# A gated recurrence followed by a long FFT convolution: weight scaling and sine arguments on GpSimd, spectral products on VectorE, a new instruction order

## Chip, core and metric

The kernel runs on one core of a Trainium2 chip, as one program. The core has five engines with a queue each: TensorE (PE in the profile, with its weight loads as PEld), VectorE (DVE), ScalarE (ACT), GpSimd (POOL) and SyncE (SP), which issues all the DMAs here. An engine works through its queue in order and waits at an instruction until what it needs is there. The metric is the device time of one execution in microseconds; lower is better.

## What is computed

Four sequences of 6272 steps and 256 channels pass through a gated recurrence and then through a multiplicative convolution as long as the sequence:

```python
sig = 1.0 / (1.0 + np.exp(-f_logit))
f = lower_bound[None, None, :] + (1.0 - lower_bound[None, None, :]) * sig
i = 1.0 - f
for t in range(S):
    h = f[:, t] * h + i[:, t] * x[:, t]
    y[:, t] = h
...
proj = y @ w_proj
x1, x2, x3 = (proj[..., :D], proj[..., D:2 * D], proj[..., 2 * D:])
X2 = np.fft.rfft(x2, n=S, axis=1)
H = np.fft.rfft(filter_fft, n=S, axis=0)[None, :, :]
x2_conv = np.fft.irfft(X2 * H, n=S, axis=1)
out = (x1 * x2_conv * x3) @ w_out
```

## The kernel before

**The work.** The transforms of length 6272 = 49 x 128 are done as matrix products with small tables of sines and cosines, in two stages each way. The work of a batch is cut into operations, each a few instructions on one engine. For the recurrence (`hgrn`), for each of 13 chunks of 512 steps: two loads, a sigmoid on ScalarE (`sig`), the product u on GpSimd (`u`, line 339), and for each half of the channels a transpose on TensorE (`su`, 351), the gate f (`f`, 364 on ScalarE or 366 on VectorE) and the scan on VectorE (`scan`, 372). The scan runs along the sequence, so the chunks follow each other. Copies of the first steps behind the end (`wrap`, 303) serve reads that run past it.

For the convolution: the projection x2 (`P`, 725, with its eviction `x2`), the first transform stage (`F1`, 737, with its eviction `A`), the second (`F2`, 795), the product with the filter's spectrum (`prod` and `pm`), the first inverse stage (`I2`, 835, with `Th`), the second (`I1`, 869), the product with the gate (`y`, 875), the output projection (`proj`, 887), its eviction `o` and the store. The 16 units of a batch each take two products. A product is *direct* when VectorE multiplies from PSUM (`prod` under the name MUL, line 816). Otherwise `prod` copies the PSUM half to SBUF in f16 (ScalarE or VectorE) and `pm` multiplies there, f16 by f16, on GpSimd (line 825). The gate x1 * x3 (`gate`) works likewise: two matmuls (`x13`, 400), a copy of x1, and then either a direct product on VectorE (MUL, line 422) or a second copy and a product on GpSimd (`z`, 431).

**Before batch 0** stands `prepare`. It loads the filter in 13 chunks, makes the tables, transforms the filter (`rot` 637, eviction `f2`; `FF1` 661, eviction `afs`; `FF2` 679, eviction `hw`) and stores its spectrum to DRAM. The tables are sines: `iotas` writes integer patterns on GpSimd, `args0` and `args1` turn them on VectorE into arguments (a multiply-add with a column of the partition's index, then `fold`, which brings them into one period), and two activations on ScalarE take the sines (563): the first set of 520 columns `v0`, then the second of 512, `v1`. `v0` gives the tables of the filter's and the data's transforms; every `FF1` matmul needs it, and all 13 `f2` evictions. `v1` gives `ID`, first needed by the last inverse stage. The `args0` and `args1` of before also compute the eleven columns (`cols`) that the tables are scaled with. Also in `prepare`, the projection weights are scaled by the column `omc` and cast (`W13`, `W2`), and `Wo` is copied, five activations on ScalarE (479, 483, 487).

**The order.** `Plan.op` records each operation with the engines it may run on and a cost; nothing sorts them in the kernel. The sequence, and for each operation its engine, is read from the string `ORDER` (`Plan.order`, lines 102 to 109): three characters hold the operation's number, its engine and its PSUM bank. `emit` walks it and issues each operation, so the string sets the order of every queue, and with `MUL` which products are direct. Four double banks of PSUM are handed out in that order.

Of the kernel before, what the change touches and what calls it, by code (L numbers as in the profile page):

```python
# [24 lines left out]
Q = 49  # L25
# [39 lines left out]
class Plan:  # L65
# [75 lines left out]
    "J4XGluJyYJ2BGsUGgSG1QJ3YGwEGhKGmYHQgJ5WJ6PG5AMrgHGSGtYMsgGkYJ9VJ7uGxYHHCJ+RGusJ8YGpWJ/FHMSGqGG3oGvYG+UG6YHZgKABHIW"
    "HNKG4YGyQHJGHAsHKSGzAG2YHigKBYG7WHLCHCsHBYKCQG/YG8GHORHRTHDYHrgHPJKDVHTDHVrHSYKHXKEAHUYKITKJHKFtKMSHWYMtAHEQKKrKGY"
    "KOKHaWKLYHFAMuYH+gH0UHcuHXSH1EH4QHeuHdYHYCHjUHbYHkYH5AHlsHfYIHgH2WMWYHgSH3GHnsHmYHsQHhCH6WHuoHoYIQgHpUHtYH7GMiYH/S"
    "HwoHvYHqEH8WKNQIBCIIUH9OHxYIZgIDqIRRICYIKEHyWITBKPoIEYKRUHzGIMsKQYKSTIiQIAYKTEIsgILYIFWIjAINYKUrKWVKVYKXTIGGKYNMXQ"
    "KZDIJYIVpI1gISYIaWIUYMYAMbUIeGMZIIWYIOSM3gMcEM4gKbXIPCMdMKaYI+gIXQKdHImSIYAIcuIbYMegMjUIfYInCIkQMkMIdYIoWIlAKcTMlM"
    "KgSMaYJHgIpGItQKerKiCIqUMnWIvoKfYIxAKhTNDgMoGIyYIgRIrMNEgIwYM5AMpOKlQI2UIhBKjrMvWIuYKnAI3YI6sKkYMzSM6YMwGKmQNPgI4E"
    "MxOKqRI7YNQgM0CIzUKsBM1KM7WI5YI0ENFAKrVKooKvTKttKpYM8GM/QNGYKuYKxDJIUM9ONbgNAAI8SNcgJMENBIKwXJKEK0WI9CJLYI/UKyvK2G"
    "K1RJBsKzYNHSK3BNRAK5WJDsJCYJAYK4YNLQNICNlgK7OJEYJFUNMANSYNmgNJKK6WJGEK+XNdANNINKgK/VNTTLAHJJYNeYK8uNXQNUDLBtK9YLDX"
    "NvgNYANVLLEWLCYMygLFHLISNwgLJVLKCNOgLNXJNYLGuLLFNfSNZILHYLPHNiUNgCLOWN6gNnANhKLMYN5gJOQNWgNjENoYLQuRtSJPANkMRuXLRY"
    "RvCLSQRwHLXSLTINxANpUMmYNsWLYKNqENyYLUQODgNtGOEgNrMLZSLVANuOLcULaCLWgNzQLdMRyWN0ALhSR0GN1IN2UN7ALmWONgN3ELiKOOgLeQ"  # L150
    "N8YLbgOFAM+gN4MLjSMqgLfALnOLrULkCOGYN9QLsMOAWN+ALoSOXgOBGN/IOYgM2gOHULpCNagOCOLwQOPAOKSLxILtWUwgOLCOQYLlgOIEOMKLyQ"
    "LuGOJML1SLzAORWL2KL0gRzROSGLqgL6UOZANCAOTOOUSOaYR1BU8gL7MU9gObWL3QOcGOVCOdOOWKOeUL4AL8WVJgVIgOfMUxgMEQL9GOgMLvgL/S"
# [825 lines left out]
```

## Time and profile before

| | |
|---|---|
| median of 3 runs | 460.52 us (459.73 to 461.34) |
| the profiled execution | 459.27 us |
| its span in the trace | 457.5 us |
| granted TensorE clock | 0.998 |
| x2 projection of batch 0, 1, 2, 3 (first line 725 matmul) | starts at 73.7, 169.8, 270.2 and 368.8 us |

The span is the time from the first instruction to the last in the trace; the execution's time includes 1.8 us around it. All times below are microseconds in that trace unless marked. A row of a group gives line, engine, operation, output and inputs, shape, count, then busy time and the mean of one instruction in ns, then idle time ahead of it with what ended it. Matmul lengths contain the end of the pipeline, so that a busy TensorE isn't a full one.

### The profile page before, as it was taken

To read this page: it belongs to the slowest core of one execution; us is meant where nothing else is said; L and a number is where in the kernel's file an instruction comes from. 1 tells how busy PE (TensorE), PEld (TensorE's weight loads), DVE (VectorE), ACT (ScalarE), POOL (GpSimd) and SP (SyncE) were. 2 spreads that over 40 slices of the span, in tenths; PEclk is the share of its full clock that TensorE was granted. 3 is DMA by queue.
4 is the path that set the end of the run, shared out by engine and by line. 5 is a ranking of instruction groups with operands and counts; after the bars stand their busy time and mean duration, and the time that the engine had idled before them with its cause. 6 is when DMAs were issued, how large, how long until landed. Compare 5 with 4: busy or idle time off the path is not lost.

```text
span 457.5 us, 14613 instructions
## 1 busy us (share of the span) xinstructions
PE 443.7 (97%) x6009; PEld 346.2 (76%) x6009; DVE 408.9 (89%) x461; ACT 399.3 (87%) x550; POOL 300.9 (66%) x274
## 2 busy tenths in 40 slices
PE   8998999999999999999999999999999999999995
PEld 6876777767766889777668889767768897677784
DVE  7599996799999993999999986999999977999873
ACT  5989998889999989989998979999989868988563
POOL 4489892289899425778996616989896405976400
PEclk9999999999999999999999999999999999999999
DMA  8999999776979997477779995487969930575176
GB/s 323 407 366 333 357 356 347 284 262 203 313 259 298 326 339 299 179 250 246 241 272 287 350 315 240 142 288 297 308 205 308 351 124 18 192 238 179 48 294 271
DMA packets 46451, 122.59 MB, mean 268 GB/s; under 512 B 4528, under 2 KB 9648, under 8 KB 46384
## 3 DMA queue, kind: packets, MB, share of 16 engines
q1 hardware_dynamic: 46384, 121.65, 75.4%
q8 instruction: 47, 0.77, 0.7%
q14 instruction: 20, 0.16, 0.1%
HBM read 86.12 MB, written 31.98 MB: 258 GB/s over the span
## 4 chain that ended last, share of the span: by engine, by line
PE 70%; DVE 15%; ACT 8%; issue 4%; POOL 2%; DVEq 0%; ACTq 0%; POOLq 0%
PE PS L400 15%; PE PS L725 9%; PE PS L835 8%; PE PS L887 8%; PE PS L351 7%; DVE HA L372 6%; PE PS L737 6%; PE PS L795 6%; DVE ys L875 4%; PE PS L637 3%; PE PS L869 3%; PE PS L661 3%; ACT fTs L364 2%; ACT HA L291 2%; PE PS L603 2%
## 5 line engine op out<-in xcount | busy, mean ns | idle before, releaser
L339 POOL TENSOR_TENSOR XT<-XT,FL 128x1024 f32<-128x1024 f32 (+1 forms) x49 | 110.0, 2247 | 52.1 <-ACT FL L337 28.9
L372 DVE TENSOR_TENSOR_SCAN HA<-fTs,HA,PS 128x512 f16<-128x512 f32 (+1 forms) x96 | 113.2, 1203 | 1.1 <-ACT fTs L364 0.2
L400 PE MATMUL PS<-HA,W 128*128 128x490 f16 (+1 forms) x416 | 102.7, 367 | 1.0 <-DVE HA L372 0.4
L825 POOL TENSOR_TENSOR PP<-HA,Hu 98x1008 f16<-98x1008 f16 x38 | 79.7, 2104 | 5.1 <-ACT HA L291 2.7
L291 ACT CAST HA<-PS 128x1024 f16<-128x1024 f32 (+1 forms) x96 | 78.2, 837 | 5.3 <-PE PS L737 2.9
L431 POOL TENSOR_TENSOR zt<-gx 128x490 f16<-128x490 f32 (+1 forms) x43 | 52.1, 1217 | 45.0 <-DVE ys L875 16.7
L816 DVE TENSOR_TENSOR PP<-PS,Hu 98x1008 f16<-98x1008 f32 x58 | 68.1, 1200 | 0.0
L875 DVE TENSOR_TENSOR ys<-PS,zt 128x1024 fp32r<-128x1024 f32 (+1 forms) x52 | 58.9, 1152 | 7.8 <-PE PS L869 4.7
L887 PE MATMUL PS<-Wo,ys 128*128 128x256 f32 x392 | 58.2, 294 | 1.6 <-DVE ys L875 1.5
L364 ACT ACTIVATE fTs<-PS,cc 128x512 f32<-128x512 f32 (+1 forms) x83 | 54.8, 675 | 5.1 <-PE PS L351 4.3
L400 PEld LDWEIGHTS <-W 128*128 128x128 f16 x416 | 34.6, 97 | 30.4 <-issue 6.8
L835 PEld LDWEIGHTS <-PP 98*128 98x128 f16 x1024 | 49.9, 97 | 9.7 <-issue 1.6
L835 PE MATMUL PS<-VV,PP 98*128 98x98 f16 x1024 | 55.9, 206 | 0.3
L887 PEld LDWEIGHTS PS<-Wo,ys 128*128 128x128 f32 x392 | 49.7, 188 | 6.6 <-DVE ys L875 2.9
L291 ACT CAST Th<-PS 128x784 f16<-128x784 f32 x59 | 48.3, 821 | 6.6 <-PE PS L835 4.6
L293 ACT ACTIVATE gx<-PS 128x490 f32<-128x490 f32 (+1 forms) x84 | 48.3, 584 | 2.5 <-PE PS L400 1.5
L337 ACT ACTIVATE FL<-FL 128x1024 f32<-128x1024 f32 (+1 forms) x49 | 49.4, 1010 | 0.0
L725 PE MATMUL PS<-W,HA 128*128 128x256 f16 x392 | 44.6, 273 | 0.2
L351 PEld LDWEIGHTS PS<-iden,FL 64*128 64x128 f32 x736 | 31.2, 138 | 16.8 <-DVE HA L372 2.9
L725 PEld LDWEIGHTS <-HA 128*128 128x128 f16 x392 | 42.9, 142 | 1.3 <-DVE HA L372 0.3
L351 PE MATMUL PS<-iden,FL 64*128 64x64 f32 x736 | 42.2, 231 | 1.6 <-DVE HA L372 0.8
L291 ACT CAST X<-PS 128x1024 f16<-128x1024 f32 (+1 forms) x31 | 32.6, 1092 | 10.3 <-PE PS L725 9.0
(130 smaller groups left out, 745.6 us busy)
## 6 DMA issues: line engine op xcount, KB each, us to landing
FL<-in_f_logit_dram SPq DMA_DIRECT2D x45, 512.0 KB, 5.5
XT<-in_x_dram SPq DMA_DIRECT2D x45, 512.0 KB, 6.4
Hu<-H SPq DMA_DIRECT2D x39, 512.0 KB, 4.8
out_dram<-osb SPq DMA_DIRECT2D x22, 512.0 KB, 4.6
out_dram<-PP SPq DMA_DIRECT2D x16, 512.0 KB, 5.3
Hx<-H SPq DMA_DIRECT2D x13, 512.0 KB, 4.4
out_dram<-HA SPq DMA_DIRECT2D x10, 512.0 KB, 5.5
X<-in_moe_filter_fft_dram SPq DMA_DIRECT2D x9, 512.0 KB, 7.2
```

The source lines that it names most:

```text
L291: nc.scalar.copy(dst, src)
L339: op("u", {"POOL": 0.1 + 0.553 * nb}, lambda e, xt=xt, ft=ft: nc.gpsimd.tensor_tensor(xt, xt, ft, op=AOP.mult), r=[("ft", k)], w=[("xt", k)])
L351: nc.tensor.transpose(bank(pb)[:, at[p] + j:at[p] + hn:nb], src[ps, j, cols], iden[ps, ps])
L364: nc.scalar.activation(fT, sT, AF.Identity, scale=by, bias=1.0)
L372: nc.vector.tensor_tensor_scan(h, fT, bank(pb)[:, 512 - hn:512 + hn], init, op0=AOP.mult, op1=AOP.add),
L400: nc.tensor.matmul(PS[:, p, 0:n], W13[:, kh, js], HA[:, HB[kh] + t0:HB[kh] + t0 + n], start=(kh == 0), stop=(kh == 1))
L725: nc.tensor.matmul(pp[:, r - r0, :], column(HB[kh], q_of(r)), W2[:, kh, :], start=(kh == 0), stop=(kh == 1))
L816: nc.vector.tensor_tensor(pr, px.unsqueeze(1).broadcast_to([TB, 2, UE, 63]), hh, op=AOP.mult)
L825: nc.gpsimd.tensor_tensor(pr, spec[:, o, :, 1:64].unsqueeze(1).broadcast_to([TB, 2, UE, 63]), hh, op=AOP.mult)
L835: nc.tensor.matmul(PS[:, ib + o, pr * TB:(pr + 1) * TB], PP[:TB, k, o, n, 2 * pr:2 * pr + 2, :], v[:TB], start=(n == 0), stop=(n == 1))
L875: nc.vector.tensor_tensor(late["ys"][:, yk, :, 0:rn * 128], PS[:, cb:cb + 2, 0:rn * 128], late["zt"][:].rearrange("p k r m -> p k (r m)") ...
L887: nc.tensor.matmul(po[:, i, :], late["ys"][:, yk, kh, i * 128:(i + 1) * 128], Wo[:, kh, :], start=(kh == 0), stop=(kh == 1))
```

## The change

1. The five scalings and copies of the weights may run on ScalarE, GpSimd or VectorE. All five now run on GpSimd.
2. The columns are an operation of their own, `cols`, on VectorE ahead of both sets. The offsets of the multiply-adds come as immediates and not from five more integer patterns, so `iotas` writes three patterns besides the index column in place of eight, and `args0` has eleven multiply-adds with one input tensor in place of five with two. `args0` stays on VectorE, `args1` goes to GpSimd.
3. `pm` may run on VectorE. The new order names it for twelve; two of these are direct and issue nothing, so ten f16 products run there: two in batch 0, one in batch 1, two in batch 2 and five in batch 3.
4. `ORDER` is new as a whole.

Counts of operations by engine that differ otherwise, read from the two strings: direct products 85 to 81; f16 products on GpSimd 43 to 37; direct gate products 61 to 54 and `z` on GpSimd 43 to 50; gate copies on ScalarE 118 to 124, on VectorE 29 to 30; `A` on VectorE 9 to 11; `afs` on VectorE 8 to 5; `f` on VectorE 21 to 18; `f2` 4 to 5, `hw` 3 to 4, `o` 3 to 5, `prod` copies 2 to 3, `Th` 5 to 4 on VectorE; `fr` on VectorE 2 to 3; `wrap` on ScalarE 3 to 5 and on GpSimd 18 to 21.

```diff
-            op("W", {"ACT": 0.6}, lambda e, kh=kh, by=by: act.activation(
-                W13[:, kh].rearrange("k (i s q) -> k i s q", i=2, s=2),
-                wp[:, kh].rearrange("k (i q s) -> k i s q", i=3, s=2)[:, 0:3:2], AF.Copy, scale=by),
+            def scaled(e, dst, src, by=by):
+                if e == "ACT":
+                    act.activation(dst, src, AF.Copy, scale=by)
+                else:
+                    (pool if e == "POOL" else dve).tensor_scalar(dst, in0=src, scalar1=by, scalar2=None, op0=AOP.mult)
+            op("W", {"ACT": 0.6, "POOL": 0.95, "DVE": 0.68}, lambda e, kh=kh, scaled=scaled: scaled(
+                e, W13[:, kh].rearrange("k (i s q) -> k i s q", i=2, s=2),
+                wp[:, kh].rearrange("k (i q s) -> k i s q", i=3, s=2)[:, 0:3:2]),
                r=["om"] + Wr(1), w=["W13"])
...
-        op("W", {"ACT": 0.5}, lambda e: act.copy(Wo[:], wo[:]), r=[("W", 0, 0)], w=["Wo"])
+        op("W", {"ACT": 0.5, "POOL": 0.7, "DVE": 0.62}, lambda e: copy(e, Wo[:], wo[:]), r=[("W", 0, 0)], w=["Wo"])
...
-                    (128, [[0, 2], [49, 2], [98, 32]], 0), (128, [[1568, 2], [0, 64]], 1568),
-                    (98, [[0, 2], [2304, Q]], 0),
-                    (98, [[1568, 2], [0, Q]], 1568), (98, [[1568, 2], [0, Q]], 0),
-                    (98, [[-1568, 2], [0, Q]], 1568), (98, [[-1568, 2], [0, Q]], 3136),
-                    (256, [[49, 256]], 0)):
+                    (128, [[0, 2], [49, 2], [98, 32]], 0), (98, [[0, 2], [2304, Q]], 0), (256, [[49, 256]], 0)):
...
+        def folded(e):
+            g = pool if e == "POOL" else dve
+
+            def fold(a, b):
+                g.tensor_scalar(v[:, a:b], in0=w[:, a:b], scalar1=1.0 / S, scalar2=big, op0=AOP.mult, op1=AOP.add)
+                g.tensor_scalar(v[:, a:b], in0=v[:, a:b], scalar1=-big, scalar2=float(S), op0=AOP.add, op1=AOP.mult)
+                g.tensor_tensor(v[:, a:b], w[:, a:b], v[:, a:b], op=AOP.subtract)
+            return g, fold
...
+        def args0(e):
+            g, fold = folded(e)
+            g.memset(cD[:, 64:65], 3136)
+            for at, n, c, k, o in [(0, 64, cD[:, 0:64], prow[:], 1568.0), (64, 1, cD[:, 64:65], prow[:], 1568.0),
+                                   (65, 63, cD[:, 65:128], prow[:], 3136.0)] + [
+                    (128 + 98 * i + Q * j, Q, cF[:, Q * j:Q * j + Q], k, o[j]) for i, (k, o) in enumerate((
+                        (kre, (1568.0, 3136.0)), (kre, (0.0, 1568.0)), (k2, (1568.0, 0.0)), (k2, (3136.0, 1568.0))))
+                    for j in range(2)]:
+                g.tensor_scalar(w[:, at:at + n], in0=c, scalar1=k, scalar2=o, op0=AOP.mult, op1=AOP.add)
+            fold(0, 520)
+
+        def args1(e):
+            g, fold = folded(e)
+            for i, (k, o) in enumerate(((kk, ore), (kim, oim))):
+                g.tensor_scalar(w[:, 520 + 256 * i:776 + 256 * i], in0=cI, scalar1=k, scalar2=o,
+                                op0=AOP.mult, op1=AOP.add)
             fold(520, 1032)
-        for i, (fn, a, b, c) in enumerate(((args0, 0, 520, 4.2), (args1, 520, 1032, 4.25))):
-            op("args", {"DVE": c}, fn, r=st + ["pint", "rot"] + ["cols0"] * i, w=[f"cols{i}", f"v{i}"])
+        op("cols", {"DVE": 4.1}, colset, r=["pint", "rot"], w=["cols1"])
+        for i, (fn, a, b, c, p) in enumerate(((args0, 0, 520, 4.0, 7.1), (args1, 520, 1032, 2.9, 3.9))):
+            op("args", {"DVE": c, "POOL": p}, fn, r=st + ["pint", "rot", "cols1"], w=[f"v{i}"])
...
-                    nc.gpsimd.tensor_tensor(
+                    (nc.vector if e == "DVE" else nc.gpsimd).tensor_tensor(
                         pr, spec[:, o, :, 1:64].unsqueeze(1).broadcast_to([TB, 2, UE, 63]), hh,
                         op=AOP.mult)
-            op("pm", {"POOL": 2.27}, late_prod,
+            op("pm", {"POOL": 2.27, "DVE": 0.62}, late_prod,
```

In the new order the queues begin so: VectorE with the rotation casts, `cols`, `args0`; GpSimd with the identity, `iotas`, the padding of the filter tile, `args1`; ScalarE with one filter cast, the sine of the first set, then eight filter evictions with the sine of the second set behind the seventh. Later in GpSimd's queue the weight scalings of batch 0's stage stand between u products: one half of `W2` and one of `W13` behind the fifth u, the other half of `W13` behind the seventh, that of `W2` behind the tenth, and `Wo` behind the eleventh of 13.

More of the change, by code (lines that the diff above doesn't have):

```diff
@@ L189 @@
[L189 to L192 removed]
+    "AAYBGgBCgAMYABIAhXACIA/gAiVBJgAsUBUgAeWA+YANIAbUBQgAcRBNgAvRBbgAtQAyUBegAqQApUAfWAaTAwWBXgArTBDABHUAOIAQYBAWBEQBig"
```

158 lines of the change are left out of this document (71 added, 87 removed).

## The prediction

> **What bounds the kernel now.** I read the page's totals and its chain of waits first, then busy time by stretches, then the timeline of the first 75 us, and last the groups by form for the prices.
>
> ```profile
> span 457.5 us, 14613 instructions
> PE 443.7 (97%) x6009; PEld 346.2 (76%) x6009; DVE 408.9 (89%) x461; ACT 399.3 (87%) x550; POOL 300.9 (66%) x274
> PE 70%; DVE 15%; ACT 8%; issue 4%; POOL 2%; DVEq 0%; ACTq 0%; POOLq 0%
> ```
>
> PE is named first, but its busy time holds pipeline ends, so I look at who has no gaps, stretch by stretch. The columns are the stretch, its length, then PE, PEld, DVE, ACT and POOL busy with instruction counts, clock, DMA share and GB/s.
>
> ```profile
> 24.00:70.00 46.00, 43.44 (x571) 34.20 (x572) 44.64 (x47) 43.78 (x65) 40.96 (x45) 1.00 0.97 352
> 85.00:140.00 55.00, 53.84 (x786) 37.56 (x784) 53.16 (x61) 51.83 (x75) 47.17 (x40) 1.00 0.76 258
> 140.00:170.00 30.00, 28.79 (x485) 23.70 (x484) 29.66 (x29) 27.36 (x40) 17.27 (x10) 1.00 0.94 315
> 181.00:236.00 55.00, 54.89 (x787) 39.36 (x788) 52.29 (x58) 51.70 (x78) 46.09 (x40) 1.00 0.68 229
> 236.00:266.00 30.00, 29.45 (x506) 23.55 (x502) 29.37 (x28) 27.54 (x41) 19.90 (x14) 1.00 0.89 302
> 300.00:362.00 62.00, 61.58 (x956) 45.80 (x955) 61.61 (x65) 58.48 (x88) 51.10 (x42) 1.00 0.85 292
> 379.00:429.00 50.00, 49.91 (x641) 35.74 (x642) 47.00 (x56) 42.87 (x62) 38.45 (x38) 1.00 0.44 141
> ```
>
> VectorE is idle for 1.8, 0.3, 2.7, 0.6, 0.4 and 3.0 us in the six stretches from 85 us on, 8.9 us in 282. In 24 to 70 us it is idle for 1.4, GpSimd for 5.0. So what a stage costs is read from the VectorE queue: work added there lengthens the run almost fully, work removed from ScalarE counts half-heartedly (it has 2.2 to 7.1 us of slack per stretch), and GpSimd matters where others wait for its products.
>
> **Two engines that block each other.** The change puts GpSimd work beside VectorE work that reads two SBUF tensors, or copies within SBUF. The timeline of the first 24 us shows what that does. Columns: start, length, engine, line, operation, count, and idle time before with its releaser.
>
> ```profile
> 3.34 1.30 DVE L537 SCALAR_TENSOR_TENSOR HA<-HA,cols 128x98 f32<-128x98 int32 x2
> 3.48 2.04 POOL L612 CAST f<-iden 128x960 fp32r<-128x960 f32 x2
> 4.67 1.13 DVE L520 TENSOR_SCALAR PP<-HA 128x520 f32<-128x520 f32 x1
> 5.46 0.39 POOL L614 CAST f<-iden 128x16 fp32r<-128x16 f32 x1
> 6.30 0.70 DVE L522 TENSOR_TENSOR PP<-HA,PP 128x520 f32<-128x520 f32 x1
> 8.99 0.14 DVE L542 TENSOR_SCALAR cols<-cols 128x1 f32<-128x1 f32 x1
> 9.82 0.64 ACT L563 ACTIVATE PP<-PP 128x520 f32<-128x520 f32 x1
> 11.28 0.15 DVE L559 TENSOR_SCALAR cols<-cols 128x1 f32<-128x1 f32 x1
> 11.35 0.42 DVE L520 TENSOR_SCALAR PP<-HA 128x512 f32<-128x512 f32 x1
> 12.26 0.69 DVE L522 TENSOR_TENSOR PP<-HA,PP 128x512 f32<-128x512 f32 x1
> 12.40 1.45 POOL L303 CAST Hx<-X 128x1024 fp32r<-128x1024 f32 x1 [6.55 <-DMA X<-in_moe_filter_fft_dram]
> 15.43 1.04 POOL L303 CAST afs<-HA 128x1024 fp32r<-128x1024 f32 x1 [1.57 <-DMA HA<-in_moe_filter_fft_dram]
> 19.25 0.69 DVE L296 CAST Hx<-X 128x1024 fp32r<-128x1024 f32 x1 [1.36 <-DMA X<-in_moe_filter_fft_dram]
> 22.19 2.15 PE L661 MATMUL PS<-D1r,f 128*128 128x256 f32 x16
> ```
>
> The same L520 instruction takes 0.42 us alone (11.35) and 1.13 us (4.67) while GpSimd's L612 casts run until 5.52; it ends 0.28 us after them. In the other direction the 1024-element cast takes 1.04 us alone and 1.45 us when VectorE's two-tensor L522 runs until 12.95. L614, 16 elements, takes 0.39 us behind L520. They alternate: each waits for the instruction of the other, then goes. In the main loop VectorE has no such instruction today, since one operand of each product comes from PSUM.
>
> The Trainium skill (SBUF — State Buffer, Who interferes with whom) says that the second to issue blocks until the first has finished, for VectorE copies in a two-port mode and for VectorE instructions with two SBUF inputs against a GpSimd read. The trace agrees (1.13 against 0.42 us, 1.45 against 1.04), and the rule speaks against this change.
>
> **Prices.** Groups by form: busy us, then mean ns.
>
> ```profile
> L816 DVE TENSOR_TENSOR PP<-PS,Hu 98x1008 f16<-98x1008 f32 x58 | 68.1, 1200 | 0.0
> L825 POOL TENSOR_TENSOR PP<-HA,Hu 98x1008 f16<-98x1008 f16 x38 | 79.7, 2104 | 5.1 <-ACT HA L291 2.7 <-DVE zp L761 1.3 <-PE PS L835 0.9
> L422 DVE TENSOR_TENSOR zt<-PS,gx 128x490 f16<-128x490 f32 x56 | 36.4, 656 | 1.1 <-ACT gx L293 0.8
> L296 DVE CAST HA<-PS 128x1024 f16<-128x1024 f32 x9 | 10.9, 1220 | 1.5 <-PE PS L737 1.1 <-POOL PP L825 0.4
> L298 DVE TENSOR_SCALAR gx<-PS 128x490 f32<-128x490 f32 x18 | 11.9, 661 | 1.0 <-POOL zt L431 0.4 <-PE PS L400 0.3
> L296 DVE CAST afs<-PS 128x512 fp32r<-128x512 f32 x3 | 2.1, 685 | 1.4 <-PE PS L661 1.4
> L366 DVE TENSOR_SCALAR fTs<-PS,cc 128x512 f32<-128x512 f32 x17 | 12.7, 744 | 1.1 <-PE PS L351 0.5 <-ACT gx L293 0.2
> L570 DVE TENSOR_SCALAR FTr<-PP,cols 128x98 fp32r<-128x98 f32 x2 | 0.6, 286 | 0.0
> L593 POOL TENSOR_SCALAR ID<-PP,cols 128x256 f16<-128x256 f32 x2 | 1.9, 943 | 0.0
> L339 POOL TENSOR_TENSOR XT<-XT,FL 128x1024 f32<-128x1024 f32 x45 | 107.1, 2382 | 45.9 <-ACT FL L337 23.0 <-ACT X L291 10.8 <-PE PS L725 9.2
> L291 ACT CAST f<-PS 128x1024 fp32r<-128x1024 f32 x9 | 10.1, 1170 | 0.8 <-PE PS L637 0.6
> ```
>
> **Step 1, the start (to the first L661 matmul at 22.19).** The 21 column instructions now come first on VectorE. One takes 0.14 to 0.15 us (L542 to L559), some 0.12 from start to start, so 2.6 us together. Then args0 makes 11 small multiply-adds from immediates in place of five (0.286 us each by L570, a little less on 49 to 64 elements: 3.1 us at most) and the same fold (0.42, 0.42, 0.69: 1.5). From 1.8 us on, where the rotation casts end, that is v0 at 9.0 us, against 7.0 now (6.30 + 0.70). Undisturbed this costs nothing: the sine ran at 9.82 anyway, and the start is then set by the last filter chunk, which lands at 19.25. But args1 now runs on GpSimd at the same moment, released by the same column set: two multiply-adds of 256 (0.94 each by L593), two folds of 512 (0.5 each at the rate of the 1024-element cast, 1.9 at that of L593) and a subtract of 512 (1.2, half of L339), 4.1 to 6.9 us, alternating with 14 VectorE instructions. If every one blocks, v0 comes at 13.1 to 15.9. ScalarE has the sine second in its order and eight filter copies behind it: 0.64 + 8 x 1.17 + 0.64 = 10.6 us, so L661 starts at 23.7 to 26.5. Bounds 0 and +4.3; I take +1.5, the whole alternation at the cheap price, since the rows show alternation each time the two met.
>
> **Step 2, to the projection of batch 0.** The rows of its end:
>
> ```profile
> 66.12 0.74 POOL L339 TENSOR_TENSOR XT<-XT,FL 128x256 f32<-128x256 f32 x1 [0.37 <-POOL mX L670]
> 66.80 1.16 POOL L303 COPY HA<-HA 128x512 f16<-128x512 f16 x2
> 68.06 0.68 POOL L650 MEMSET X<- 128x384 f16 x1
> 72.73 0.85 DVE L372 TENSOR_TENSOR_SCAN HA<-fTs,HA,PS 128x128 f16<-128x128 f32 x2
> 73.83 10.81 PE PS L725 x98
> ```
>
> ScalarE loses five weight scalings and takes three afs copies and two f evaluations from VectorE (one f of 128 columns, about half), which is 3 x 0.685 + 1.5 x 0.744 = 3.2 us less on VectorE before the last scan: the projection could start at 70.6. GpSimd pays: the scalings of W13 (512 elements, twice 1.9 by L593), of W2 (256, 0.94 twice) and the copy of Wo (0.5) are 6.2 us; at the rate of a plain cast they are 2.1. Two wrap copies more ahead of the last u add 1.2 (66.80), the memset of X2's tail columns (68.06) moves ahead of it as well, +0.7, and that of X2's gaps to before the stretch, -1.7. So its last u, done at 66.86, has 2.3 to 6.4 us more ahead of it, and 5.0 us of idle to take them in, which are not all in the right places. The projection follows the last u by some 2 us at best. Between 70.6 and 75.3 I take 72.8: -1.0, bounds -3.2 and +1.5. Behind those scalings in GpSimd's queue stand the u products, and for them transposes, scans and the projection wait.
>
> **Step 3, from there to the end.** By the entries of the order string, VectorE gets ten f16 products (2 more name VectorE where the product is direct, and issue nothing), and loses four direct products, six direct gate products, one Th copy and one f; it gains two A copies, two gate copies, two output copies and one spectrum copy. An f16 product reads the bytes of L522 (2 x 1008 x 2 against 2 x 512 x 4): 0.69 us if bytes count, 1.2 (L816, as many elements) if elements do. I take 0.69, as L522 is the only row with both operands in SBUF. The sum is 10 x 0.69 - 4 x 1.20 - 6 x 0.656 + 2 x 1.22 + 2 x 0.661 + 0.6 for the other five = +2.5 us. GpSimd loses six products of 2.1 and gets seven gate products; that frees some 4 us where it isn't the bound. ScalarE gains about as much as VectorE.
>
> The Trainium skill (VectorE: DVE Perf Modes, the perf-mode tier table) gives two-tensor operations on 2-byte SBUF data twice the rate; no run here shows it yet. By it the sum stays; by the one-element rate it is 5 us more.
>
> **Step 4, blocking in the main loop.** GpSimd is busy 47 of 55 us and 38 of 50 where the ten products fall. Four of them (batch 1's eleventh unit, batch 2's third and last, batch 3's fourth) stand in the list right behind a GpSimd product of 2.1 us, as its twin; on average half is left, 4 x 1.05 = +4.2. For the others I take 0. Bounds 0 and 10 x 2.1. What is queued behind them on VectorE are scans and PSUM evictions, and for those PE waits.
>
> **Step 5, the new order.** It can close at most VectorE's 8.9 us of gaps, or open others. I take a third, -3.0, bounds -8.9 and +3.
>
> Sum: 1.5 - 1.0 + 2.5 + 4.2 - 3.0 = +4.2 us on the profiled execution's 459.27, so 463.5; the runs' median, 460.52, lies 1.25 above that execution, so **464.7 us**.
>
> **Rivals.**
> - *The balance pays* (other side): blocking stays rare since the list puts the products where GpSimd waits, and the weights fit into its 5.0 us of idle. Then 0 - 3.2 + 2.5 + 0 - 3.0 = -3.7: 456.8. For it: VectorE and ScalarE are both relieved in the fullest stage; against: the trace shows blocking at every meeting. It decides if v0 is done before 10 us and the projection starts before 71.
> - *Elements count*: an f16 product takes 1.2 us, +5.3 on the forecast: 470.0. For it L816 and L522, which both take about 1.2 to 1.3 ns an element; against, the bytes.
> - *GpSimd bounds the first stage*: the weights at L593's rate push the last u, +1.5 in place of -1.0, and the start goes to +3: 464.7 + 2.5 + 1.5 = 468.7.
> - *A wash*: start and stage cancel, no blocking in the loop: 1.5 - 1.0 + 2.5 + 0 - 3.0 = 0, so 460.5.
>
> **Chances.** Forecast 0.42, balance 0.25, elements 0.12, GpSimd 0.08, wash 0.13. The runs spread over 0.35%, so about 0.3% (1.4 us) can be told from no change. Faster 0.25, same 0.13, slower 0.62. The range runs from 457.5, into the balance case, to 470.5, past the elements case.
>
> **What would show it.** Step 1: start of the first L661 matmul, and VectorE's small multiply-adds stretched beside GpSimd's. Step 2: the group that scales W on GpSimd at 0.9 and 1.9 us, and the first L725 matmul near 74. Steps 3 and 4: the new VectorE product group, its shortest (0.69 or 1.2) and how far its mean lies above that. Wrong I am if its mean equals its minimum, or if VectorE's gaps after 85 us shrink by more than 6 us.

## The result and the profile after

The changed kernel takes 474.69 us (median of 6 runs, 469.20 to 475.47) against 460.21 us before (6 runs, 458.49 to 461.34): ratio 1.0287, 95% interval 1.0249 to 1.0324. Five of its six executions lie between 473.11 and 475.47 us, with a granted TensorE clock of 0.988 to 0.991; the one of 469.20 had 0.996, and no trace of it was kept. The profiled execution after took 473.11 us, 13.84 us more than the one before. The forecast was 464.7 us, and its range ended at 470.5.

Line numbers move by 3 to 8 in the changed kernel: the direct product is 824, `pm` 833, the `FF1` matmul 669, the projection 733, the inverse stages 843 and 877. Line 808 is `slot`, a small sum on GpSimd, one for each unit. From the page after, the span, the engines and the shares of the chain of waits:

```profile
span 471.2 us, 14628 instructions
PE 447.5 (95%) x6009; PEld 349.2 (74%) x6009; DVE 424.5 (90%) x462; ACT 398.9 (85%) x556; POOL 309.1 (66%) x283
PE 63%; DVE 16%; ACT 9%; POOL 5%; issue 5%; DVEq 0%; ACTq 0%; POOLq 0%
```

VectorE is busy 15.6 us longer, with one instruction more. Where that falls is read from busy time by stretches, here one stretch for each batch, from its projection to the next one's (the last to the last `I2`); first before, then after. Columns as in the prediction's table of stretches.

```profile
73.67:169.78 96.11, 93.74 (x1367) 72.05 (x1366) 89.69 (x96) 87.24 (x122) 65.90 (x51) 1.00 0.85 292
169.78:270.22 100.44, 99.58 (x1445) 77.50 (x1441) 91.23 (x95) 93.55 (x133) 70.87 (x54) 1.00 0.78 270
270.22:368.82 98.60, 97.73 (x1425) 76.27 (x1424) 92.68 (x97) 90.42 (x129) 72.12 (x57) 1.00 0.77 269
368.82:428.62 59.80, 59.71 (x726) 45.33 (x724) 53.51 (x61) 48.82 (x69) 38.45 (x38) 1.00 0.41 134
```

```profile
73.93:170.27 96.34, 93.64 (x1367) 72.16 (x1366) 90.73 (x96) 87.71 (x124) 65.92 (x52) 1.00 0.87 297
170.27:271.07 100.80, 99.93 (x1444) 77.61 (x1442) 92.59 (x97) 94.00 (x135) 72.09 (x55) 1.00 0.79 270
271.07:379.90 108.83, 101.09 (x1424) 78.92 (x1424) 100.87 (x97) 91.75 (x131) 68.93 (x56) 0.97 0.65 229
379.90:442.95 63.05, 60.10 (x721) 44.94 (x719) 55.53 (x61) 51.36 (x74) 40.12 (x39) 1.00 0.44 144
```

The projection of batch 0 starts 0.26 us later than before, so the first stage is even. Batches 0 and 1 lose 0.23 and 0.36 us, batch 2 loses 10.23, batch 3 3.25; behind the last `I2` 0.6 us come back (the spans differ by 13.7). In batch 2 the number of VectorE's instructions is the same (97), yet it is busy 8.19 us longer, while the mean granted clock falls to 0.97.

The new f16 products on VectorE, by tile (count, then shortest/median/longest in ns):

```profile
L833 DVE TENSOR_TENSOR PP<-HA,Hu x9: 674/1020/4710, 112.1 to 441.0; 98x1008 f16<-98x1008 f16 x9
L833 DVE TENSOR_TENSOR PP<-HA,Hx x1: 4674/4674/4674, 341.4 to 341.4; 98x1008 f16<-98x1008 f16 x1
```

The same instruction takes 0.67 us at its shortest and 4.71 at its longest. One after another the ten take 1.02, 0.68, 0.69, 4.71, 4.67, 1.47, 0.67, 2.88, 0.69 and 1.72 us, 19.2 in all: 6.8 of work (10 x 0.68) and 12.4 of waiting. Both long ones stand in batch 2 (`pm.2.5` at 295.18, `pm.2.31` at 341.43): 8.0 us of waiting. The timeline around the first:

```profile
293.54 2.11 POOL L833 TENSOR_TENSOR PP<-HA,Hu 98x1008 f16<-98x1008 f16 x1
294.62 0.64 DVE L422 TENSOR_TENSOR zt<-PS,gx 128x490 f16<-128x490 f32 x1
295.18 4.71 DVE L833 TENSOR_TENSOR PP<-HA,Hu 98x1008 f16<-98x1008 f16 x1
295.60 1.24 POOL L431 TENSOR_TENSOR zt<-gx 128x490 f16<-128x490 f32 x1
296.79 0.35 POOL L808 TENSOR_TENSOR PP<-zp 98x32 f16<-98x32 f16 x1
296.99 2.36 POOL L339 TENSOR_TENSOR XT<-XT,FL 128x1024 f32<-128x1024 f32 x1
297.54 1.08 PE L400 MATMUL PS<-HA,W 128*128 128x490 f16 x4
299.82 0.74 DVE L366 TENSOR_SCALAR fTs<-PS,cc 128x512 f32<-128x512 f32 x1
301.92 0.69 PE L803 MATMUL PS<-HA,FT 64*128 64x256 f16 x8 [3.31 <-DVE HA L372]
```

VectorE's product was issued while GpSimd's product (to 295.65) ran. It did not go when that ended: three more GpSimd instructions went ahead of it, none of them stretched, and it ended at 299.89, 0.54 us behind the last (299.35). The gate value f, the scans and then TensorE waited: 3.31 us without a matmul. Behind the gap, the clock, by stretches:

```profile
298.62:302.33 3.71, 0.41 (x8) 0.34 (x8) 3.67 (x4) 1.97 (x3) 1.49 (x2) 1.00 0.68 224
302.33:305.74 3.41, 3.41 (x31) 2.59 (x28) 2.92 (x3) 1.82 (x2) 0.46 (x1) 0.50 0.52 205
305.74:309.15 3.41, 3.41 (x56) 2.12 (x54) 2.75 (x4) 2.65 (x5) 0.97 (x1) 1.00 0.51 159
```

For 3.41 us the granted clock is half (31 matmuls against 56 in the next 3.41). The wait at 341.43 does the same: 3.60 us without a matmul and 3.41 us at half clock. Before the change TensorE had no gap over 1.5 us.

At the start, columns and multiply-adds are stretched beside GpSimd's casts and its `args1`, and the first sine runs at 11.82 in place of 9.82; still the first `FF1` matmul (L669) begins at 22.54, 0.35 later. In both traces that is 3.1 us behind the landing of the last filter chunk (19.13 before, 19.40 after), so most of the 0.35 is the landing:

```profile
2.60 1.97 POOL L620 CAST f<-iden 128x960 fp32r<-128x960 f32 x2
2.67 0.95 DVE L538 SCALAR_TENSOR_TENSOR cols<-cols 128x1 f32<-128x1 f32 x1
6.53 3.59 DVE L559 TENSOR_SCALAR HA<-HA,cols 128x49 f32<-128x49 int32 x8
7.37 1.27 POOL L525 TENSOR_TENSOR PP<-HA,PP 128x512 f32<-128x512 f32 x1
11.82 0.64 ACT L571 ACTIVATE PP<-PP 128x520 f32<-128x520 f32 x1 [3.61 <-DVE PP L525]
22.54 0.74 PE L669 MATMUL PS<-D1r,f 128*128 128x256 f32 x4
```

### The profile page after: what moved, and what is told of

Its sections match the earlier page's. It is cut to its first block, busy times and chain, and to the rows that moved or that the text cites. A ratio compares the mean times of both kernels' runs of the same rounds, so it can differ in the third digit from the quotient of the medians.

```text
span 471.2 us, 14628 instructions
## 1 busy us (share of the span) xinstructions
PE 447.5 (95%) x6009; PEld 349.2 (74%) x6009; DVE 424.5 (90%) x462; ACT 398.9 (85%) x556; POOL 309.1 (66%) x283
## 4 chain that ended last, share of the span: by engine, by line
PE 63%; DVE 16%; ACT 9%; POOL 5%; issue 5%; DVEq 0%; ACTq 0%; POOLq 0%
PE PS L400 15%; PE PS L733 9%; PE PS L843 8%; PE PS L895 8%; PE PS L351 6%; PE PS L803 5%; PE PS L745 5%; DVE HA L372 5%; DVE ys L883 5%; PE PS L877 3%; POOL XT L339 2%; ACT f L291 2%; DVE PP L824 2%; PE PS L669 2%; ACT HA L291 2%
## 5 line engine op out<-in xcount | busy, mean ns | idle before, releaser
L431 POOL TENSOR_TENSOR zt<-gx 128x490 f16<-128x490 f32 (+1 forms) x50 | 61.9, 1243 | 39.3 <-DVE ys L883 17.4
L833 POOL TENSOR_TENSOR PP<-HA,Hu 98x1008 f16<-98x1008 f16 x33 | 69.8, 2118 | 10.6 <-issue 5.4
L824 DVE TENSOR_TENSOR PP<-PS,Hu 98x1008 f16<-98x1008 f32 x54 | 63.4, 1199 | 0.7 <-POOL zt L431 0.5
L364 ACT ACTIVATE fTs<-PS,cc 128x512 f32<-128x512 f32 (+1 forms) x86 | 56.3, 675 | 7.5 <-DVE HA L372 4.4
L843 PEld LDWEIGHTS <-PP 98*128 98x128 f16 x1024 | 51.2, 98 | 13.0 <-issue 2.5
L843 PE MATMUL PS<-VV,PP 98*128 98x98 f16 x1024 | 57.6, 209 | 3.0 <-DVE PP L833 1.1
L293 ACT ACTIVATE gx<-PS 128x490 f32<-128x490 f32 (+1 forms) x85 | 49.3, 584 | 5.9 <-PE PS L400 3.9
L803 PE MATMUL PS<-HA,FT 64*128 64x256 f16 x512 | 37.6, 271 | 3.4 <-DVE HA L372 3.3
```

The costliest lines, as they stand in the source:

```text
L431: nc.gpsimd.tensor_tensor(zd(), xs(0), xs(1), op=AOP.mult)
L824: nc.vector.tensor_tensor(pr, px.unsqueeze(1).broadcast_to([TB, 2, UE, 63]), hh, op=AOP.mult)
L833: (nc.vector if e == "DVE" else nc.gpsimd).tensor_tensor(pr, spec[:, o, :, 1:64].unsqueeze(1).broadcast_to([TB, 2, UE, 63]), hh, op=AOP.mult)
L843: nc.tensor.matmul(PS[:, ib + o, pr * TB:(pr + 1) * TB], PP[:TB, k, o, n, 2 * pr:2 * pr + 2, :], v[:TB], start=(n == 0), stop=(n == 1))
```

## The experiments

In the expectations, A is the theory that VectorE's f16 products, waiting behind GpSimd, cause the loss; its rivals are named there. Most edits change the engine of single entries of the order, everything else staying in place:

```diff
-            yield word // 64, self.ENGINES[word // 8 % 8], word % 8
+            i = word // 64
+            yield i, MOVED.get(i, self.ENGINES[word // 8 % 8]), word % 8
```

**The ten products, taken back or added.** First all ten back on GpSimd, then only the two long ones, then the kernel before with ten of its products moved to VectorE (with the change's lines that let `pm` run there).

```diff
+MOVED = {515: 'POOL', 524: 'POOL', 1074: 'POOL', 1526: 'POOL', 1672: 'POOL', 2073: 'POOL', 2121: 'POOL', 2149: 'POOL', 2211: 'POOL', 2213: 'POOL'}
```

> The changed kernel with all ten f16 products issued on GpSimd at the same places of the order. Theory A (blocking): the changed kernel's ten products take 19.1 us on VectorE where 6.8 would do unblocked, and hold up scans and evictions; without them most of the 14.5 us goes, 462 to 466, with the long gaps of batch 2 gone. Rival B (load and order): the new order is badly balanced, blocking costs little; VectorE loses 10 x 0.68 but GpSimd gets 10 x 2.1 in a place not planned for it, so 470 to 480.

Measured: 476.90 us, ratio 1.0348 (1.0329 to 1.0368). Batch 2 gets shorter (from the first `I1` matmul of batch 1 to that of batch 2, 101.1 against 109.5 us), but batch 3 takes 68.35 against 63.05, with TensorE gaps of 1.81 and 4.02 us; 3.41 us at half clock follow the first, 6.82 us begin within the second. The gain that A expected did not come, and the time lies in the range of its rival: TensorE waited 9.0 us for GpSimd's products and `slot` sums, against 0.8 in the change. GpSimd is busy for only 47.9 of the 68.35 us of batch 3, so its products were late at their places in the queue, while in total it had time left.

```diff
+MOVED = {1526: 'POOL', 1672: 'POOL'}   # pm.2.5, pm.2.31
```

> The changed kernel with only the two f16 products of batch 2 (4.71 and 4.67 us in its trace) on GpSimd. Theory A: those two account for 8.0 us of waiting and batch 2 lost 10.2 us against before; 465 to 468. Rival B: two products are worth 2 x 0.68 us of VectorE, less GpSimd's 4.2 us; 473 to 476.

Measured: 466.48 us, ratio 1.0129 (1.0106 to 1.0151), 8.2 us faster than the change and inside A's range. TensorE has no gap over 1.5 us, and the clock stays whole until the last stores. Its batches 2 and 3:

```profile
271.06:371.57 100.51, 98.09 (x1424) 76.59 (x1423) 91.61 (x95) 91.37 (x130) 72.94 (x58) 1.00 0.70 247
371.57:434.59 63.02, 60.09 (x722) 44.93 (x719) 55.51 (x61) 50.88 (x74) 40.09 (x39) 1.00 0.42 144
```

Batch 2 gains 8.32 us: VectorE is busy 9.26 us less (the waits, 8.0, and the products' own 1.4) and idle 0.94 more. So the two products are the cause of 8.3 of the 10.2 us that batch 2 lost, and VectorE's time accounts for all of it; a loss by the half clock on top doesn't show. Batch 3 is as long as in the change.

```diff
+MOVED = {514: 'DVE', 523: 'DVE', 1073: 'DVE', 1525: 'DVE', 1671: 'DVE', 2072: 'DVE', 2120: 'DVE', 2146: 'DVE', 2203: 'DVE', 2212: 'DVE'}
```

> The kernel before with ten of its 43 f16 products moved to VectorE (eight of them the same ones), nothing else. Theory A: each meets a busy GpSimd; waits of 0 to 4 us each, slower than 460.2 by 5 to 13 us. Rival B: the products are harmless, 10 x 0.68 us on VectorE against 10 x 2.1 on GpSimd: 458 to 464.

Measured: 466.19 us, ratio 1.0119 (1.0091 to 1.0146). Only one product waits long (2.60 us); the ten take 8.76 in all, 2.0 of it waiting, and a TensorE gap of 1.95 us is followed by 3.41 us at half clock. So ten such products, eight of them the same, cost 5.8 us in the old order with little waiting. That is inside what A expected, but the waiting is small beside the 6.8 us of work that VectorE gets here with nothing taken off it, so this run does not speak for A; rival B, by which the products are harmless, falls as well.

**The weights and the sine arguments.** First the five scalings back on ScalarE and `args1` back on VectorE in the changed kernel; then the scalings alone on GpSimd in the kernel before.

```diff
+MOVED = {7: 'ACT', 8: 'ACT', 9: 'ACT', 10: 'ACT', 11: 'ACT'}   # W
```

> The changed kernel with the five weight scalings back on ScalarE at the same places. In the changed trace they take 5.9 us on GpSimd and its last u of batch 0 starts 3.1 us later, yet the projection of batch 0 only 0.3 us later. Theory A: nothing to be had here, 473 to 476. Rival C (GpSimd holds up the first stage): 470 to 472, with the projection of batch 0 at 71 to 72 us instead of 73.9.

```diff
+MOVED = {16: 'DVE'}   # args1
```

> The changed kernel with both sets of sine arguments on VectorE. In the changed trace its eight small multiply-adds take 3.6 us beside GpSimd's second set and the first set is done at 11.8 us, yet the first L669 matmul starts at 22.5, 0.3 us later than before. Theory A: the start is set by the last filter chunk, so nothing is to be had: 473 to 476. Rival (the start matters): first matmul at 22 or before and 1 to 2 us less in all.

```diff
-            op("W", {"ACT": 0.6}, lambda e, kh=kh, by=by: act.activation(
+            op("W", {"POOL": 0.6, "ACT": 0.6}, lambda e, kh=kh, by=by: pool.tensor_scalar(
...
+MOVED = {7: 'POOL', 8: 'POOL', 9: 'POOL', 10: 'POOL', 11: 'POOL'}
```

> The kernel before with its five weight scalings on GpSimd and nothing else changed. By step 2 as the prediction has it, ScalarE's relief is worth about 1 us: 459 to 460. If the first matmul and the last u set the stage, nothing: 460.2 to 460.9. If GpSimd's 5.9 us push the last u: 461.5 to 463.

Measured: 476.56 us (ratio 1.0338, 1.0314 to 1.0362), 472.34 us (1.0217, 1.0143 to 1.0291) and, on the kernel before, 465.10 us (1.0100, 1.0079 to 1.0121). The first lies just past A's range, and C falls: with the scalings on ScalarE the changed kernel's projection of batch 0 starts at 76.28, 2.35 later. About 1.0 of that is the filter's last chunk, which landed at 20.48 in this trace and not at 19.40. With `args1` on VectorE the first `FF1` matmul starts at 23.09, 0.55 later, and here the chunk landed at 20.07, so nothing is left of it. The time of that kernel lies just below A's 473, but can't be told from that of the change, as the intervals overlap: two of its four executions took 469.05 and 470.02 us, the others 474.65 and 475.21. The traces of both still hold the two TensorE gaps of 3.3 and 3.6 us. The third lies past the last of its alternatives: in the old order the scalings on GpSimd cost 4.6 us. Two rows of GpSimd's timeline before; then the same stretch with the scalings on it, and the first projection matmul:

```profile
36.64 1.72 POOL L645 MEMSET X<- 128x1920 f16 x1
38.61 2.40 POOL L339 TENSOR_TENSOR XT<-XT,FL 128x1024 f32<-128x1024 f32 x1
```

```profile
36.77 1.96 POOL L488 TENSOR_SCALAR W<-HA,cc 128x256 f16<-128x256 f32 x2
38.63 1.71 POOL L651 MEMSET X<- 128x1920 f16 x1
40.60 2.39 POOL L343 TENSOR_TENSOR XT<-XT,FL 128x1024 f32<-128x1024 f32 x1
42.96 1.62 POOL L483 TENSOR_SCALAR W<-HA,cc 128x512 f16<-128x512 f32 x1
77.71 1.48 PE L731 MATMUL PS<-W,HA 128*128 128x256 f16 x11
```

The u product that began at 38.61 before begins at 40.60, the last u at 70.16 in place of 66.12, and the projection at 77.71 in place of 73.67, 4.04 later. At the places that the old order gives them, the scalings are dear in that stage. In the change something in the rest of the new order pays for them (the `afs` copies on ScalarE, the memset ahead of the stretch, other places for the scalings); which of these was not separated.

**What a product waits for.** Four kernels compute nothing of the reference; they measure one VectorE product beside GpSimd instructions that are back to back. The first has all of it on 128 partitions.

> The two engines by themselves, nothing of the reference: VectorE f16 products of 128 x 1008 with both inputs in SBUF beside runs of six GpSimd instructions that need not wait (products of 1024, of mixed sizes, copies), products that read what ScalarE made before, and VectorE products with one input in PSUM. Theory A1 (alternation): a product waits for the GpSimd instruction that runs and then goes, at most 2.4 us over its 0.68, and the next GpSimd instruction is longer by 0.68. Theory A2 (starving): while GpSimd has its next instruction ready, it keeps the port, and a product waits for two or more instructions, up to the whole run of six (14 us). The product from PSUM takes 1.2 us in every case.

Measured: alone a product takes 0.68 us. One product issued beside six u-like products takes 2.78 us: the GpSimd instruction in hand ends, the product goes, and the next GpSimd instruction is stretched by 0.44 us. Four products in a row take 10.99, so they alternate one by one. With one operand in PSUM four take 4.93, 1.2 each, and GpSimd isn't stretched. The longest single product of this run took 2.87. So by this run a product can wait for one instruction, not four.

In the kernel the spectral products and `slot` sums of GpSimd use 98 partitions, the others 128. The second of the four varies that.

```python
loop = ((f16, 1008, 98), (f32, 490, 128), (f16, 32, 98), (f32, 1024, 128), (f32, 490, 128), (f32, 490, 128))
stage(loop, 98)
stage([(fn, n, 128) for fn, n, r in loop], 98)
```

> The two engines by themselves again, nothing of the reference: one VectorE f16 product on 98 partitions that becomes ready about 1.5 us into a run of six GpSimd instructions. Runs: the main loop's mixture (98 partitions 1008 f16, 128 x 490, 98 x 32, 128 x 1024, then 490 twice) twice; the same sizes all on 128, then all on 98 partitions; 1024 f32 alternating 98 and 128, then all 128; 490 f32 all 128, alternating, and with only the first on 98. The run before showed alternation when every GpSimd instruction covers 128 partitions, while the changed kernel's product waited through four. Theory S (rows): GpSimd's units for the rows that a 98-partition instruction leaves out go on to the next one, so that some unit always holds the port; waits of 2 to 4 instructions where 98 and 128 are mixed, at most one more instruction where all are alike. Rival (sizes or types): the waits follow the sizes, alike in the mixture and in the runs of the same sizes on 128 or on 98.

Measured: in the loop's mixture the product takes 6.43 us, both times, and gets in behind the fifth of six instructions; with the same sizes all on 128 partitions 1.58, all on 98 1.59. Of 490 f32 alternating between 98 and 128 partitions 4.03, all on 128 1.68. Two mixtures speak against a simple rule: 1024 f32 alternating let the product go at 1.60, and 490 with only the first on 98 at 1.72.

```python
for late in (64, 256, 384, 512, 640):      # moment of issue, all on 128 partitions
    stage(chain, 98, late)                 # 1008, copy 512, 32, copy 512, 1024
for late in (256, 512):
    stage(plain, 98, late)                 # 1008, 490, 32, 1024
stage([(fn, n, 98 if fn is f16 else r) for fn, n, r in plain], 98, 512)
stage([(fn, n, 98 if i == 0 else r) for i, (fn, n, r) in enumerate(plain)], 98, 512)
```

> No part of the reference: the same VectorE product of 98x1008 f16, issued later and later in the first GpSimd instruction of the chain behind pm.2.31 (all on 128 partitions), then beside a chain with an f32 product of 490 in place of the first copy, and the same with 98 partitions for the f16 instructions, or for the first alone. If what matters is how near to the end of the first instruction the product is issued when a short copy follows, the product takes 1.6 us when early and over 4 when late, in the chain with copies alone. If unequal partition counts alone matter (theory S), the seven stages on 128 partitions take 0.7 to 1.6, falling as the product is issued later, and the last two 3 to 5. Then the 4.69 us of pm.2.31 with full rows stay open.

Measured, on 128 partitions: 1.30, 1.15, 1.04, 0.94 and 0.83 us beside the chain with copies, 1.15 and 0.94 beside the other. With the f16 instructions on 98 partitions, or the first alone: 4.61. The timeline of the second stage of `plain` and of the last stage, which differ in that one number:

```profile
56.16 2.09 POOL L71 TENSOR_TENSOR gh<-ha,vb 128x1008 f16<-128x1008 f16 x1 [1.28 <-DVE ha L64]
57.84 0.94 DVE L80 TENSOR_TENSOR vo<-va,vb 98x1008 f16<-98x1008 f16 x1 [1.83 <-ACT va L68]
58.20 1.65 POOL L74 TENSOR_TENSOR go<-ga,gb 128x490 f32<-128x490 f32 x1
59.82 0.24 POOL L71 TENSOR_TENSOR gh<-ha,vb 128x32 f16<-128x32 f16 x1
```

```profile
71.29 2.09 POOL L71 TENSOR_TENSOR gh<-ha,vb 98x1008 f16<-98x1008 f16 x1 [1.89 <-DVE ha L64]
72.98 4.61 DVE L80 TENSOR_TENSOR vo<-va,vb 98x1008 f16<-98x1008 f16 x1 [1.83 <-ACT va L68]
73.34 1.21 POOL L74 TENSOR_TENSOR go<-ga,gb 128x490 f32<-128x490 f32 x1
74.51 0.24 POOL L71 TENSOR_TENSOR gh<-ha,vb 128x32 f16<-128x32 f16 x1
74.71 2.33 POOL L74 TENSOR_TENSOR go<-ga,gb 128x1024 f32<-128x1024 f32 x1
```

Above, the product ends at 58.78 and the 490 is stretched to 1.65. Below, it waits for the whole chain, and ends 0.55 us behind its last instruction, as at 295.18 in the kernel. So a spectral product of GpSimd on 98 partitions, followed at once by work on 128, can keep VectorE out for several instructions, here to the end of the chain. It does not do so each time. In the changed kernel the product at 405.22 is also issued while one on 98 partitions runs, with a `z` on 128 next, and goes behind that one instruction:

```profile
404.04 2.10 POOL L833 TENSOR_TENSOR PP<-HA,Hu 98x1008 f16<-98x1008 f16 x1
405.22 1.47 DVE L833 TENSOR_TENSOR PP<-HA,Hu 98x1008 f16<-98x1008 f16 x1
406.10 1.67 POOL L431 TENSOR_TENSOR zt<-gx 128x490 f16<-128x490 f32 x1
```

What decides between 1.47 and 4.71 us there, no run shows.

**The same in the kernel.** The products on either engine, the `slot` sums and the sums' inputs go over all 128 partitions (the additional rows hold values that nothing reads):

```diff
-            px = PS[:TB, pb:pb + 2, 0:2 * n]
+            px = PS[:, pb:pb + 2, 0:2 * n]
...
-            PP[:TB, k, :, :, :, 0], zp[:TB, u // NA % 2, :, :, 0, ka:ka + UE],
+            PP[:, k, :, :, :, 0], zp[:, u // NA % 2, :, :, 0, ka:ka + UE],
...
+                    full = A[:, ka:ka + UE].rearrange("p i r k -> p (i r k)").rearrange(
+                        "p (o i k) -> p o i k", o=2, k=64)
...
-                        pr, spec[:, o, :, 1:64].unsqueeze(1).broadcast_to([TB, 2, UE, 63]), hh,
+                        PP[:, k, o, :, :, 1:64],
+                        full[:, o, :, 1:64].unsqueeze(1).broadcast_to([128, 2, UE, 63]),
...
```

> The changed kernel, with its f16 products, the sums of the slot column and the products they add up taken on all 128 partitions in place of 98 (the rows above 98 are read by nothing), so that all of GpSimd's main loop covers 128. Theory S: the f16 products of batch 2 wait for one instruction (at most 2.4 us over 0.68) in place of four, no TensorE gap over 3 us there, 464 to 468. Rival: nothing changes, 473 to 476.

Measured: 469.16 us, ratio 1.0172 (1.0114 to 1.0230), 5.5 us faster than the change and between the two expectations. One execution of the change took 469.20 too, with the clock (0.996) that this run's trace has with one gap left, so a long wait may at times be missing without any edit, and the time alone would be weak evidence. The products' lengths say more; by tile:

```profile
L835 DVE TENSOR_TENSOR PP<-HA,Hu x9: 673/694/1717, 112.5 to 436.3; 128x1008 f16<-128x1008 f16 x9
L835 DVE TENSOR_TENSOR PP<-HA,Hx x1: 4686/4686/4686, 337.9 to 337.9; 128x1008 f16<-128x1008 f16 x1
```

`pm.2.5` falls from 4.71 to 1.01 us, although it is issued at the same moment as before, 1.64 us into GpSimd's product, with the same instructions behind that; `pm.0.16` from 1.02 to 0.68, `pm.3.19` from 2.88 to 1.70. `pm.2.31` stays at 4.69, behind a chain that is now all on 128 partitions:

```profile
336.34 2.11 POOL L835 TENSOR_TENSOR PP<-HA,Hx 128x1008 f16<-128x1008 f16 x1
338.39 0.61 POOL L303 COPY HA<-HA 128x512 f16<-128x512 f16 x1
338.96 0.34 POOL L808 TENSOR_TENSOR PP<-zp 128x32 f16<-128x32 f16 x1
339.15 0.61 POOL L303 COPY HA<-HA 128x512 f16<-128x512 f16 x1
339.72 2.34 POOL L339 TENSOR_TENSOR XT<-XT,FL 128x1024 f32<-128x1024 f32 x1
```

That chain by itself, in the third of the four measuring kernels:

> No part of the reference: one VectorE product of 98x1008 f16 issued beside five GpSimd instructions, in eight mixtures. The chain behind pm.2.31 in the kernel with full rows was product 1008, f16 copy 512, slot 32, f16 copy 512, then 1024 f32, all on 128 partitions, and the product took 4.69 us. If the f16 copies let GpSimd's units run apart as unequal partition counts do (theory S), the product takes 4 to 5 us in the first, second and fifth mixture only where copies or unequal lengths stand, and 1.6 to 2.8 where there are 1008, 32, 1024 alone. If the length of the first instruction alone sets it, all eight give 2.3 to 2.8. If it is a matter of the kernel's other traffic, the first two give 1.6 to 2.8 and the cause stays open.

Measured: 1.58 us on 128 partitions, 5.20 with the products on 98, and 1.58 or 1.59 in all others. Neither this nor the moment of issue (0.83 to 1.30 above) brings back the 4.69, so that instance stays open. Two differences were not tried: VectorE's product covers 98 partitions in these stages and 128 in the kernel with full rows, and TensorE is idle beside them.

**A better version?** Two tries. In one, `pm.2.5` and `pm.3.19` are direct from PSUM, the former moved behind the batch's first `I2`, with `pm.2.31` on GpSimd (an entry on the right of `LATER` is issued behind the one on its left); in the other, full rows with `pm.2.31` and `pm.3.19` on GpSimd.

```diff
+MOVED = {1525: 'MUL', 2148: 'MUL', 1672: 'POOL'}
+LATER = {1511: 1525}
```

> The changed kernel with three of its blocked f16 products out of the way: batch 2's third and batch 3's tenth unit's first half are direct products from PSUM on VectorE (1.2 us, no second SBUF input, no copy on ScalarE), batch 2's last is on GpSimd. Theory A: against the run with two products on GpSimd (466.5) the tail loses 2.2 us of waiting and gains 0.5 of product: 463.5 to 466, and no half-clock stretch before the end. Rival B (load alone): 1.2 for 0.68 us on VectorE, twice: 467 to 468.

```diff
+MOVED = {1672: 'POOL', 2149: 'POOL'}   # on the kernel with full rows
```

> The kernel after with its products on all 128 partitions, and pm.2.31 and pm.3.19 given back to GpSimd. If waiting of VectorE's products is the cause, the 4.69 and 1.70 us instances (5.0 us over 0.68 each) and the last gap of TensorE (3.62 us) with its half clock go: 463.5 to 465.5. If GpSimd is full and hands the two products' 2 us on to the u products, 467 to 470.

Measured: 466.04 us (1.0109, 1.0071 to 1.0148) and 466.10 us (1.0128, 1.0100 to 1.0155). Neither quite reaches its expectation. In the second the remaining eight products take 7.61 us, 2.2 over their work, and no TensorE gap over 1.5 us is left in either. Neither can be told from the run with two products on GpSimd (466.48), and no version that was run beats the kernel before.

## Why the prediction was wrong, step by step

**The bound** held: what VectorE got, the run got. From the projection of batch 0 to the last `I2`, VectorE's busy time goes from 327.11 to 339.72 us (sums of the two tables), +12.6, and its idle time from 27.8 to 29.3, +1.5; with 0.26 ahead and -0.6 behind, that is the 13.7 us between the spans.

**Step 1** (+1.5) came out at +0.35. Its mechanism is there (L538 at 0.95 for 0.16, the sine 2.0 us later), but it fell into the wait for the last filter chunk, the cover that the step had named for the undisturbed case only: the first `FF1` matmul stands 3.1 us behind that landing before and after.

**Step 2** (-1.0) came out at -0.1 (0.26 less 0.35). The scalings took 5.9 us on GpSimd, near the dear price of 6.2. Alone, in the old order, they cost 4.0 us, more than the step's upper bound, and the rest of the new order returned as much. That the step ended inside its bounds is in part luck, as it had no term of that size, and the rival that saw GpSimd as the bound of the first stage had a true mechanism and no loss.

**Step 3**, the price of 0.69 us for an f16 product, was right: the four undisturbed ones took 0.67 to 0.69. Elements do not count, and that rival falls, although its 470.0 lies nearest to the result. (By the prediction's own prices it adds 10 x 0.51 = 5.1 us and not 5.3, so 469.8; and L522's 0.69 us for 512 elements are 1.35 ns each, not 1.2 to 1.3.) The Trainium skill (VectorE: DVE Perf Modes, the perf-mode tier table) gave twice the rate to two-tensor operations on 2-byte data, and the trace agrees: 0.68 us for 1008 elements where the 4-byte PSUM form takes 1.20. The sum of +2.5 was right as well: from the projection to the end VectorE is busy 14.5 us longer (12.6 to the last `I2`, 1.9 behind it), and less 12.4 of waiting 2.1 are left. It counts two gate copies where the order has one more, and leaves out the one more `prod` copy, 0.66 for 0.69.

**Step 4 failed.** The prediction took four meetings, with "half" of one GpSimd product each, "4 x 1.05 = +4.2". The products waited 12.4 us. Of the four named, one waited for nothing, one 0.8 us, and the two of batch 2 4.0 each; the six put at 0 waited 3.6 together. The rule behind it, that each waits for the one instruction of the other, was read from the start of the kernel, where all instructions have 128 partitions. The measuring kernels show that rule where all of GpSimd's work is on 128 partitions (2.9 us at most), and show it gone, 4.6 to 6.4 us, when a spectral product on 98 partitions is followed by work on 128, as in the main loop; in the kernel itself such a pair sometimes held VectorE up and sometimes did not (4.71 and 1.47 us). The two waits also held up the scans and gate products behind them, hence TensorE's gaps of 3.3 and 3.6 us. Giving those two products back to GpSimd returns 8.2 of the 14.5 us.

The Trainium skill (SBUF — State Buffer, Who interferes with whom) lets the second to issue wait until the first finishes; the runs show more, a wait through four to five instructions. A sentence in the Trainium skill (GPSIMD Engine Reference, 2.1 Instruction dispatch) bears on it: each GpSimd core serves 16 partitions and starts the next instruction as soon as its own share is done. By that, cores with nothing to do at 98 partitions would run ahead, and the engine as a whole not let go between two instructions. The runs fit it in most mixtures, but not in 1024 f32 alternating (1.60), not in 490 with only the first on 98 (1.72), and not in `pm.2.31` on full rows (4.69), so it is an explanation and not shown.

**Step 5** (-3.0) did not come: VectorE's gaps grew by 1.5 us. Had steps 1 to 3 and 5 stood, they would have given 0; measured, they give about +1.4 (13.8 less 12.4).

**The range** was cut at 470.5, past the elements case, while step 4's own upper bound of 10 x 2.1 reached 481.5 (464.7 less 4.2 plus 21). With that bound in it, the range would have held.

**Open**: the 4.69 us of `pm.2.31` on full rows, why a product on 98 partitions holds VectorE up at one place and not at another, and the last 6 us. With the two long products back on GpSimd, 3.2 of these lie in batch 3 and 1.9 in batch 2; 4.4 us of waiting remain in its eight products (9.8 less 8 x 0.68). How much of the 6 us these waits cost, and how much the order, was not separated.

## What to carry to other kernels

A VectorE product with both inputs in SBUF can cost, besides its own time, the rest of the GpSimd instruction in hand (1.0 to 1.7 us in all for 0.68, at three of the ten here). If GpSimd's instructions use unequal numbers of partitions, bound it by a whole chain and not by one instruction (up to 4.7 us in the kernel), or keep an operand in PSUM (1.17 to 1.22 us in all 81 such products of the changed kernel). Before work is moved to an engine with spare time on average, look at which of its queue's instructions then come late: in the old order five small scalings and copies, 5.9 us beside 5.0 us of idle, delayed the last u product by 4.0.

## What the runs showed of the hardware

- A VectorE product waited through up to five GpSimd instructions (6.43 us against 0.68 alone); in one chain a single instruction on 98 partitions in place of 128 made the difference (4.61 against 0.94). The same pair of a product on 98 and a `z` on 128 held a product up in the kernel at 295.18 (4.71) and not at 405.22 (1.47).
- In the change, TensorE gaps of 3.31 and 3.60 us were followed by 3.41 us at half clock each, and so were gaps of 1.81 and 1.95 in other runs; behind one of 3.31, with the scalings back on ScalarE, and from within one of 4.02 it lasted 6.8. A gap of 2.01 us, in the kernel before with the scalings on GpSimd, had none behind it. The Trainium skill (TensorE: Matmul & The Clock Gate, Why this matters for your kernels) warns of gaps over about 3 us; here shorter ones did it at times.
